# A scheduled attention and two-layer network kernel: later value loads in the planner's order, and the old state added on TensorE in early chunks

## The chip, the core and the metric

The kernel runs on one core of a Trainium2 chip. The metric is device microseconds of one execution, taken as the median of several runs. A core has TensorE (matmul, called PE in the profile, with PEld for its weight loads), VectorE (DVE), ScalarE (ACT), GpSimd (POOL) and SyncE (SP), which here does nothing but issue DMAs. Each engine works through its own list of instructions in the order in which the program wrote them. An instruction that waits for another engine or for a DMA holds up everything behind it on its own engine.

## What is computed

A linear attention with a state of 40x40 per head runs over 768 positions for 4 x 8 heads, and its output goes through two dense networks:

```python
for t in range(S):
    y[:, :, t] = np.einsum('bhd,bhde->bhe', rt, state)
    Sa = np.einsum('bhde,bhe->bhd', state, at)
    state_decay = state * wt[:, :, None, :] - np.einsum('bhd,bhe->bhde', Sa, bt)
    state = state_decay + np.einsum('bhd,bhe->bhde', vt, kt)
x = y.transpose(0, 2, 1, 3).reshape(B * S, H * D)              # 3072 x 320
h = np.maximum(np.maximum(x @ w1, x @ w2), x @ w3) @ w_out     # 768 wide
out = (h @ w_a * (h @ w_b)) @ w_out2                           # 1536 wide
```

## The kernel before

**Stages.** The 768 positions are cut into 24 chunks of 32, and two chunks make a pair (12 pairs). For each pair, `prep` loads decay factors, keys and the vectors a, scans the decays (L395, L399), multiplies keys and vectors by them, makes a block of products on TensorE (L446 for the first five pairs, L428 for the others), and solves small triangular systems on VectorE and GpSimd (`solve`, L500 to L502). Its results travel through DRAM because they change partitions. The products go out as BD and come back as BU for the solve (L460, L466). The first result goes out as TD and comes back as TT (L472, L476), the second out as ED and back as NB (L481, L484). All of these are DMAs in SP's queue.

**The chain.** `chain(c)` does chunk c, and each step needs the one before:

- z (L617, needs the operands ZR, which hold the state and a value load), then Zs on ScalarE (L623)
- "half" (L631, needs TT), then Zy on ScalarE (L635)
- u (L644, needs NB), then four copies into XX on ScalarE (L654)
- the state product (L664, function `smm`, two halves x = 0 and 1, 16 matmuls each, reads XX and YR)
- a VectorE add of the product to the state ST (L672), in every fourth chunk a VectorE multiplication of ST by a decay (L676), and copies from ST into ZR for the next z (L683 on ScalarE or L684 on VectorE, whichever the planner takes)

ST is also transposed on TensorE for the next chunk (L593). Off this chain the chunk's output is made by L690, L702, L706, L720 and L724. It goes to DRAM and comes back as xf (`gather`, L733 to L740).

**Dense networks.** `moe_a(p)` runs the first network on a pair (L828 and L853 to L857 on TensorE), writes X2D to DRAM (L863, L864), and needs weights split into two parts by `weights_a` (VectorE L750 to L753 and matmuls L777, L778, L780). `stage_b` splits the weights of the second network and stores them in DRAM. `moe_b` runs the second network in six tiles (L982 to L992) after all attention is done.

**Order.** Nothing is ordered by hand. Each step is handed to a planner (`Plan.op`) with its engine, an assumed duration, its operands and a priority. `Plan.run` plays all of this through on assumed durations and writes each engine's instructions in the order that comes out. The attention has the best priority, `moe_a` a lower one. For a DMA the planner assumes a time on SP, a time `lat` until its data is there, and a delay `pre` before SP may take it once its operands are free; these only decide the order, and no instruction waits for them on the chip. Where an operation has a second way (`alt`), the planner picks the engine. When the planner finds TensorE too idle for its clock it inserts a **fill**: a 128x128 matmul whose result nobody reads (`P.keep`, L276 in the profile). Fills stand in TensorE's list like any other work.

**Loads of a chunk.** `vload(d, 0)` loads values into ZR, `vload(d, 1)` loads values into XX (both L557). RB is L562, XT L564 and YL L568. Each overwrites what the previous chunk's matmuls still read, so SP's wait for such a load ends when that matmul is done.

Of the kernel before, what the change touches and what calls it, by code (L numbers as in the profile page):

```python
# [22 lines left out]
GP = [0, 64]  # L23
NYR, NZR = 2, 1
NW = 9
LV = 9
KG = 5
NSPL = 2
DMIN = 0.4
# [208 lines left out]
def body(nc, tc, ia, out_ap):  # L238
# [8 lines left out]
    def dv(n, ps=False):  # L247
        return 0.15 + n * 0.00105 if ps else 0.12 + n * 0.0014

    def ac(n):  # L250
        return 0.17 + n * 0.0009
# [2 lines left out]
        return 0.4 + n * 0.0023  # L254

    def dma(fn, nbytes, r=(), w=(), pri=0.0, pre=1.2):
        return op("SP", max(DMIN, nbytes / 300e3), fn, r=r, w=w, pri=pri, lat=2.0 + nbytes / 200e3, pre=pre)

    def adma(fn, nbytes, r=(), w=(), pri=0.0, after=()):

# [279 lines left out]
    def chain(c):  # L540
# [8 lines left out]
        def vload(d, q, after=()):  # L549

            for i in range(2):
                t, w = ((lambda i=i: (ZR[d % NZR][64 - GP[i]:96 - GP[i], i].rearrange("p u x d -> p (u x d)"), ia["vz"][d, i]), ("ZRv", d % NZR, i)),
                        (lambda i=i: (XX[64 * i:64 * i + 32].rearrange("p u g d -> p (u g d)"), ia["vx"][d, i]), ("XXv", i)))[q]
                if after:
                    adma(lambda w_, t=t: A.dma_start(*t()), 82e3, w=[w], pri=pr, after=after)
                else:
                    dma(lambda w_, t=t: SP.dma_start(*t()), 82e3, w=[w], pri=pr)  # L557

        vload(c, 0)
        for g in range(2):  # L560
            r0 = GP[g]
            dma(lambda w_, g=g, r0=r0: SP.dma_start(RB[40 * g:40 * g + 40, g].rearrange("p u t -> p (u t)"), ia["rb"][c, g]),  # L562
                82e3, w=[("RB", g)], pri=pr)
        dma(lambda w_: SP.dma_start(XT[0:80, :, 0, :], ia["vt"][c].rearrange("p (u t) -> p u t", t=32)),  # L564
            328e3, w=[("XTv", 0), ("XTv", 1)], pri=pr)
        for x in range(2):
            y0 = 64 * (1 - x)
            dma(lambda w_, x=x, y0=y0: SP.dma_start(YL[y0:y0 + 40, x].rearrange("p u g t -> p (u g t)"), ia["ry"][c, x]),  # L568
                82e3, w=[("YLr", x)], pri=pr)
        vload(c, 1)  # L570

        for hf in range(2):
# [84 lines left out]
        for x in range(2):  # L657
            pn = ("a", "s", c, x)

            def smm(w_, x=x, pn=pn):  # L660
                ps = bank[w_[pn]]
                for u in range(8):
                    for g in range(2):
                        T.matmul(ps[64 * g:64 * g + 40, u * 40:u * 40 + 40],  # L664
                                 Y_[64 * x:64 * x + 64, x, u, g], XX[64 * x:64 * x + 64, u, g], start=True, stop=True)

            if c == NCH - 1:
                continue
            op("PE", 0.82, smm, r=[("YRy", yb, x, hf) for hf in range(2)] + [("XXu", x, pq) for pq in range(2)] + [("XXv", x)],
               w=[pn], ps=[pn], act=0.22, pri=pr)  # L670
            sv = ST[0:104, :, 1 - x, 0:40]
            op("DVE", dv(320, True), lambda w_, sv=sv, pn=pn: V.tensor_tensor(  # L672
                sv, bank[w_[pn]][0:104, 0:320].rearrange("p (u d) -> p u d", d=40), sv, ALU.add),
               r=[pn], w=["ST", ("STx", x)], fin=[pn], pri=pr)
            if cc and p % 2:
                op("DVE", 0.74, lambda w_, sv=sv, x=x: V.tensor_tensor(  # L676
                    sv, sv, P_[0:104, cc].rearrange("p (u x) s -> p u x s", x=2)[:, :, x, 32:33].to_broadcast([104, 8, 40]), ALU.mult),
# [1 line left out]
            for g in range(2):  # L679
                r0 = GP[g]  # L680
                o_ = ZR[z2][r0:r0 + 40, g, :, 1 - x]
                i_ = ST[r0:r0 + 40, :, 1 - x, 0:40]
                op("ACT", ac(320), lambda w_, o_=o_, i_=i_: A.activation(o_, i_, AF.Copy), r=[("STx", x)], w=[("ZRs", z2, g)], pri=pr,  # L683
                   alt=[("DVE", 0.47, lambda w_, o_=o_, i_=i_: V.tensor_copy(o_, i_))])  # L684

        px = ("a", "xt", c)

# [575 lines left out]
```

## Time and profile before

| | |
|---|---|
| median of 3 runs | 1092.65 us (1087.15 to 1097.81) |
| the profiled execution, its own time | 1090.93 us |
| its span in the profile | 1088.7 us |
| mean granted TensorE clock | 0.975 |
| PE, DVE, ACT, POOL busy | 95%, 60%, 44%, 21% |
| instructions in the trace | 34319 |

The profile has one execution. The span runs from its first to its last instruction, and 2.2 us of its time lie outside the span. A busy PE in the profile can be doing fills. "Issue" is idle time for which the profile shows no cause.

### The profile page before, as it was taken

To read this page: it belongs to the slowest core of one execution; us is meant where nothing else is said; L and a number is where in the kernel's file an instruction comes from. 1 tells how busy PE (TensorE), PEld (TensorE's weight loads), DVE (VectorE), ACT (ScalarE), POOL (GpSimd) and SP (SyncE) were. 2 spreads that over 40 slices of the span, in tenths; PEclk is the share of its full clock that TensorE was granted. 3 is DMA by queue.
4 is the path that set the end of the run, shared out by engine and by line. 5 is a ranking of instruction groups with operands and counts; after the bars stand their busy time and mean duration, and the time that the engine had idled before them with its cause. 6 is when DMAs were issued, how large, how long until landed. Compare 5 with 4: busy or idle time off the path is not lost.

```text
span 1088.7 us, 34319 instructions
## 1 busy us (share of the span) xinstructions
PE 1034.9 (95%) x14868; PEld 936.6 (86%) x14868; DVE 654.0 (60%) x1091; ACT 480.7 (44%) x1115; POOL 230.1 (21%) x198
## 2 busy tenths in 40 slices
PE   8999789999899998999899999999999999999997
PEld 7878778988798888898889899988888888888886
DVE  7896698968797875989587633475223232332222
ACT  6246546555647373847375532343222232222221
POOL 4441365533423222323320200011000000000000
PEclk9998899899999989999899999999999999999999
DMA  8846875656666847577655547742002000000000
GB/s 272 199 96 161 173 158 126 157 140 167 158 167 153 190 117 189 136 168 166 150 135 149 136 122 204 200 104 62 10 1 54 1 25 1 2 25 1 25 1 27
DMA packets 173437, 123.10 MB, mean 113 GB/s; under 512 B 122464, under 2 KB 147168, under 8 KB 172320
## 3 DMA queue, kind: packets, MB, share of 16 engines
q1 hardware_dynamic: 170688, 116.41, 43.4%
q10 hardware_dynamic: 2592, 4.42, 1.2%
q8 instruction: 119, 1.95, 0.8%
q14 instruction: 38, 0.31, 0.1%
HBM read 93.07 MB, written 27.72 MB: 111 GB/s over the span
## 4 chain that ended last, share of the span: by engine, by line
PE 70%; DVE 12%; DMA 8%; issue 4%; SPq 3%; ACT 1%; POOL 1%; DVEq 0%; POOLq 0%; ACTq 0%
PE bank L982 24%; PE bank L828 11%; PE bank L992 4%; PE bank L990 4%; PE bank L991 4%; PE bank L276 3%; DMA NB<-ED 2%; PE bank L664 2%; PE bank L720 2%; PE bank L644 2%; PE bank L702 2%; PE bank L853 2%; PE bank L854 1%; PE bank L617 1%; PE bank L855 1%
## 5 line engine op out<-in xcount | busy, mean ns | idle before, releaser
L1000 DVE TENSOR_TENSOR bas<-bank,bas 128x512 f32<-128x512 f32 x72 | 49.7, 691 | 188.8 <-PE bank L982 179.8
L982 PE MATMUL bank<-bxhi,bw 128*128 128x512 f32 x576 | 156.3, 393 | 0.0
L982 PEld LDWEIGHTS bank<-bxhi,bw 128*128 128x128 f32 x576 | 106.2, 188 | 20.8
L999 ACT ACTIVATE bas<-bank 128x512 f32<-128x512 f32 x72 | 43.0, 598 | 148.2 <-PE bank L982 144.2
L1002 ACT ACTIVATE bgh<-bas 128x512 fp32r<-128x512 f32 x72 | 45.5, 633 | 125.5 <-DVE bas L1000 125.5
L828 PE MATMUL bank<-xhi,whi 128*128 128x256 f32 x432 | 95.5, 303 | 0.0
L843 DVE TENSOR_TENSOR hm<-bank,hm 128x512 f32<-128x512 f32 x72 | 49.5, 688 | 67.0 <-PE bank L828 66.1
L982 PE MATMUL bank<-bxlo,bw 128*128 128x512 f32 x288 | 89.8, 393 | 0.0
L992 PE MATMUL bank<-bo,bgl 128*128 128x320 f32 x288 | 89.0, 309 | 0.4 <-DVE bgl L1003 0.4
L990 PE MATMUL bank<-bo,bgh 128*128 128x320 f32 x288 | 89.0, 309 | 0.0
L991 PE MATMUL bank<-bo,bgh 128*128 128x320 f32 x288 | 88.9, 309 | 0.0
L828 PE MATMUL bank<-xlo,whi 128*128 128x256 f32 x432 | 88.5, 287 | 0.0
L828 PE MATMUL bank<-xhi,wlo 128*128 128x256 f32 x432 | 88.2, 286 | 0.0
L413 POOL TENSOR_TENSOR ZL<-ZL,Pp 64x512 f32<-64x512 f32 x44 | 58.7, 1334 | 85.4 <-DVE Pp L395 75.0
L1003 DVE TENSOR_TENSOR bgl<-bas,bgh 128x512 fp32r<-128x512 f32 x72 | 49.8, 691 | 43.0 <-ACT bgh L1002 42.8
L276 PE MATMUL bank<-con 128*128 128x128 f32 x494 | 69.2, 293 | 4.0 <-DMA con<-in_con_dram 2.8
L828 PEld LDWEIGHTS bank<-xhi,whi 128*128 128x128 f32 x432 | 67.6, 194 | 2.6
L276 PEld LDWEIGHTS bank<-con 128*128 128x128 f32 x494 | 62.9, 203 | 7.6 <-ACT bank L344 2.8
L828 PEld LDWEIGHTS bank<-xlo,whi 128*128 128x128 f32 x432 | 68.6, 195 | 0.0
L828 PEld LDWEIGHTS bank<-xhi,wlo 128*128 128x128 f32 x432 | 68.4, 195 | 0.0
L982 PEld LDWEIGHTS bank<-bxlo,bw 128*128 128x128 f32 x288 | 54.1, 188 | 12.2
L828 PE MATMUL bank<-xt,wt 128*128 128x256 f32 x216 | 62.0, 287 | 0.0
(181 smaller groups left out, 2446.0 us busy)
## 6 DMA issues: line engine op xcount, KB each, us to landing
wraw<-in_wpb_dram SPq DMA_DIRECT2D x18, 480.0 KB
KT<-in_kb_dram SPq DMA_DIRECT2D x20, 384.0 KB
Pp<-in_wf_dram SPq DMA_DIRECT2D x10, 528.0 KB
Rp<-in_wr_dram SPq DMA_DIRECT2D x10, 528.0 KB
wraw<-in_wpa_dram SPq DMA_DIRECT2D x12, 384.0 KB
bw<-WD SPq DMA_DIRECT2D x9, 512.0 KB
WD<-wraw ACTq DMA_DIRECT2D x18, 240.0 KB
WD<-wca SPq DMA_DIRECT2D x18, 240.0 KB
```

Source lines behind the costliest of these rows:

```text
L276: P.keep = lambda b: T.matmul(bank[b][:, 0:128], ident, ident, start=True, stop=True)
L413: op("POOL", po(512), lambda w_, cc=cc, g=g, r0=r0: G.tensor_tensor(Z_[r0:r0 + 64, cc, g], Z_[r0:r0 + 64, cc, g], P_[r0:r0 + 64, cc, :, 0: ...
L828: T.matmul(ps, w, x, start=(i == 0), stop=(i == 7))
L843: op("DVE", dv(512, True), lambda w_, pn=pn: V.tensor_tensor(f(hm), bank[w_[pn]], f(hm), ALU.max), r=[pn], w=["hm"], fin=[pn], pri=ep)
L982: T.matmul(ps, w, x, start=(k == 0), stop=(k == 7))
L990: T.matmul(o, gh[:, c], oh, start=ff == 0, stop=False)
L991: T.matmul(o, gh[:, c], ol, start=False, stop=False)
L992: T.matmul(o, gl[:, c], oh, start=False, stop=ff == 11)
L999: op("ACT", ac(512), lambda w_, j=j, pa=pa: A.activation(tb["as", j], bank[w_[pa]], AF.Copy), r=[pa], w=[("bas", j)], fin=[pa], pri=ep)
L1000: op("DVE", dv(512, True), lambda w_, j=j, pb=pb: V.tensor_tensor(tb["as", j], bank[w_[pb]], tb["as", j], ALU.mult), r=[pb], w=[("bas", j) ...
L1002: op("ACT", ac(512), lambda w_, j=j, k=k: A.activation(tb["gh", k], tb["as", j], AF.Copy), r=[("bas", j)], w=[("gh", k)], pri=ep)
L1003: op("DVE", dv(512), lambda w_, j=j, k=k: V.tensor_tensor(tb["gl", k], tb["as", j], tb["gh", k], ALU.subtract), r=[("bas", j), ("gh", k)], ...
```

## The change

Three things change in the program, and the planner then writes a new order for every engine.

- The planner's assumed time until a DMA's data is there goes from 2.0 us + bytes / 200 GB/s to 1.4 us + bytes / 250 GB/s, for all DMAs that SP issues. Loads of a chunk get a longer `pre`: values into ZR 2.5 us and into XX 6.0 us, RB and XT 4.0 us, YL 5.0 us, each 1.2 us before.
- In chunks 1 to 8 (`early`) the old state joins the product in the same PSUM bank: a matmul of the identity with ST (104 partitions x 320 columns) comes first, the 16 matmuls of each half add to it, and ScalarE copies the sum into ST. The VectorE add is gone there. Later chunks keep it.
- The copies from ST into ZR are always ScalarE's. VectorE no longer has them as a second way.

```diff
-        return op("SP", max(DMIN, nbytes / 300e3), fn, r=r, w=w, pri=pri, lat=2.0 + nbytes / 200e3, pre=pre)
+        return op("SP", max(DMIN, nbytes / 300e3), fn, r=r, w=w, pri=pri, lat=1.4 + nbytes / 250e3, pre=pre)
...
-                    dma(lambda w_, t=t: SP.dma_start(*t()), 82e3, w=[w], pri=pr)
+                    dma(lambda w_, t=t: SP.dma_start(*t()), 82e3, w=[w], pri=pr, pre=[2.5, 6.0][q] if d else 1.2)
...
-                82e3, w=[("RB", g)], pri=pr)
+                82e3, w=[("RB", g)], pri=pr, pre=4.0 if c else 1.2)
...
+            early = 0 < c < NACC
+            if early:
+
+                op("PE", 0.6, lambda w_, x=x, pn=pn: T.matmul(bank[w_[pn]][0:104, 0:320], ident[0:104, 0:104], ST[0:104, :, 1 - x, 0:40], start=True, stop=False, skip_group_check=True),
+                   r=["ST", ("STx", x), "con"], w=[pn], ps=[pn], act=0.9, pri=pr)
+            op("PE", 0.82, lambda w_, smm=smm, early=early: smm(w_, early), r=[("YRy", yb, x, hf) for hf in range(2)] + [("XXu", x, pq) for pq in range(2)] + [("XXv", x)],
+               w=[pn], ps=[] if early else [pn], act=0.22, pri=pr)
             sv = ST[0:104, :, 1 - x, 0:40]
-            op("DVE", dv(320, True), lambda w_, sv=sv, pn=pn: V.tensor_tensor(
-                sv, bank[w_[pn]][0:104, 0:320].rearrange("p (u d) -> p u d", d=40), sv, ALU.add),
-               r=[pn], w=["ST", ("STx", x)], fin=[pn], pri=pr)
+            if early:
+                op("ACT", ac(320), lambda w_, sv=sv, pn=pn: A.activation(sv, bank[w_[pn]][0:104, 0:320].rearrange("p (u d) -> p u d", d=40), AF.Copy),
+                   r=[pn], w=["ST", ("STx", x)], fin=[pn], pri=pr)
+            else:
+                op("DVE", dv(320, True), lambda w_, sv=sv, pn=pn: V.tensor_tensor(
+                    sv, bank[w_[pn]][0:104, 0:320].rearrange("p (u d) -> p u d", d=40), sv, ALU.add),
+                   r=[pn], w=["ST", ("STx", x)], fin=[pn], pri=pr)
...
-                op("ACT", ac(320), lambda w_, o_=o_, i_=i_: A.activation(o_, i_, AF.Copy), r=[("STx", x)], w=[("ZRs", z2, g)], pri=pr,
-                   alt=[("DVE", 0.47, lambda w_, o_=o_, i_=i_: V.tensor_copy(o_, i_))])
+                op("ACT", ac(320), lambda w_, o_=o_, i_=i_: A.activation(o_, i_, AF.Copy), r=[("STx", x)], w=[("ZRs", z2, g)], pri=pr)
```

In the changed file line numbers are 1 higher from L27 on and 9 higher from about L690 on; the state product is L665 there, the new matmul L673, a fill L277.

TensorE, chunk 2 (third chunk), from the fills ahead of u to the next chunk's z. Before:

```order
L276 MATMUL bank_64<-con 128x128 x7
L644 MATMUL bank_64<-Zy,NB_145 32x40 x32
L276 MATMUL bank_69<-con 128x128 x5
L664 MATMUL bank_69<-XX,YR_131 40x40 x16
L276 MATMUL bank_66<-con 128x128
L664 MATMUL bank_66<-XX,YR_131 40x40 x16
L690 MATMUL bank_65<-con,XU 80x128 x4
L276 MATMUL bank_70<-con 128x128
L593 MATMUL bank_70<-con,ST 128x104 x4
L593 MATMUL bank_68<-con,ST 128x104 x4
L702 MATMUL bank_63<-RB,XT 64x64 x16
L617 MATMUL bank_67<-ZR_136,ZL_127 32x40 x32
```

The same place with the change:

```order
L277 MATMUL bank_68<-con 128x128 x5
L645 MATMUL bank_68<-Zy,NB_145 32x40 x32
L277 MATMUL bank_70<-con 128x128 x5
L665 MATMUL bank_67<-XX,YR_131 40x40 x16
L277 MATMUL bank_70<-con 128x128
L699 MATMUL bank_70<-con,XU 80x128 x4
L673 MATMUL bank_63<-ST,con 104x320
L665 MATMUL bank_63<-XX,YR_131 40x40 x16
L711 MATMUL bank_65<-RB,XT 64x64 x16
L673 MATMUL bank_64<-ST,con 104x320
L594 MATMUL bank_68<-con,ST 128x104 x4
L618 MATMUL bank_67<-ZR_136,ZL_127 32x40 x32
```

Three fills are gone and two state matmuls (L673) are in, the first for the second half of this chunk, the second already for chunk 3.

SP's queue at pair 3 (fourth pair; BD_71 and BU are its products on the way to the solve, XX the values of chunk 5). Before:

```order
L460 DMA BD_71<-ZL_126 32x16x32
L740 DMA xf<-XD_81 64x256 x2
L760 DMA wraw<-in_wpa_dram 128x768
L460 DMA BD_71<-ZL_126 32x16x32
L375 DMA Rp<-in_wr_dram 128x1056
L460 DMA BD_71<-ZL_126 32x16x32 x2
L557 DMA XX<-in_vx_dram 32x640 x2
L466 DMA BU<-BD_71 64x512
L466 DMA BU<-BD_71 64x496
L564 DMA XT<-in_vt_dram 80x16x32
L562 DMA RB<-in_rb_dram 40x512 x2
```

With the change:

```order
L461 DMA BD_71<-ZL_126 32x16x32
L376 DMA Rp<-in_wr_dram 128x1056
L461 DMA BD_71<-ZL_126 32x16x32
L769 DMA wraw<-in_wpa_dram 128x768
L461 DMA BD_71<-ZL_126 32x16x32 x2
L749 DMA xf<-XD_81 64x256
L467 DMA BU<-BD_71 64x512
L467 DMA BU<-BD_71 64x496
L558 DMA XX<-in_vx_dram 32x640
L383 DMA ZL_128<-in_aa_dram 48x2x512 x2
L565 DMA XT<-in_vt_dram 80x16x32
L563 DMA RB<-in_rb_dram 40x512 x2
```

The value load XX moved from ahead of BU to behind it.

SP's queue at pair 5 (chunk 10 is its first), from TT to NB. Before:

```order
L476 DMA TT_141<-TD_76 32x16x32 x4
L375 DMA Pp_121<-in_wf_dram 128x1056
L375 DMA Rp<-in_wr_dram 128x1056
L738 DMA xf<-XD_80 128x2x256
L740 DMA xf<-XD_80 64x256 x2
L863 DMA X2D_85<-x2s 128x512
L864 DMA X2D_85<-x2s 64x256
L481 DMA ED_79<-TC 64x128 x2
L920 DMA wraw<-in_wpb_dram 128x960
L928 DMA WD<-wca 128x480
L460 DMA BD_71<-ZL_126 32x16x32 x2
L484 DMA NB_145<-ED_79 16x16x16 x4
```

With the change:

```order
L376 DMA Pp_121<-in_wf_dram 128x1056
L569 DMA YL<-in_ry_dram 40x512 x2
L937 DMA WD<-wca 128x480
L929 DMA wraw<-in_wpb_dram 128x960
L477 DMA TT_141<-TD_76 32x16x32 x4
L371 DMA KT_125<-in_kb_dram 48x2048
L482 DMA ED_79<-TC 64x128 x2
L371 DMA KT_125<-in_kb_dram 48x2048
L485 DMA NB_145<-ED_79 16x16x16 x4
```

Ten DMAs between TT and NB, besides ED, became two. Counted over TensorE's whole list, fills go from 247 to 193, 53 of the 54 before the z of chunk 5 (211 to 158), and 16 state matmuls are new, 9 of them before that z. Between "half" and u of chunk 10 stand 80 matmuls of L828 and 16 of L853 to L857 before; with the change 16, 16, and 16 of L428.

## Rows read from the trace of the kernel before

**Rows 1.** The page: busy time of each engine, share of the span, instructions.
```profile
PE 1034.9 (95%) x14868; PEld 936.6 (86%) x14868; DVE 654.0 (60%) x1091; ACT 480.7 (44%) x1115; POOL 230.1 (21%) x198
```

**Rows 2.** Stretches: length, PE, PEld, DVE, ACT, POOL busy, PEclk, DMA share, GB/s.
```profile
26.00:80.40 54.40, 50.67 (x746) 42.80 (x746) 47.88 (x83) 20.50 (x55) 24.61 (x21) 1.00 0.66 150
...
174.20:689.30 515.10, 484.90 (x9910) 454.94 (x9911) 382.22 (x642) 282.72 (x695) 148.86 (x127) 0.97 0.64 157
689.40:1088.70 399.30, 392.78 (x2018) 343.01 (x2016) 134.31 (x214) 108.44 (x188) 6.87 (x6) 0.99 0.11 30
```

**Rows 3.** What PE waited for, 0 to 650 us: total us, times, longest.
```profile
PE bank L644 <- DMA NB<-ED: 13.6, 9, 3.2
PE bank L631 <- DMA TT<-TD: 5.9, 11, 2.2
```

**Rows 4.** PE instructions by form: busy us, mean ns (a fill is two).
```profile
L276 PE MATMUL bank<-con 128*128 128x128 f32 x494 | 69.2, 293 | 4.0 <-DMA con<-in_con_dram 2.8 <-DVE XY L724 1.1
```

**Rows 5.** Timeline of PE, and its last row from the chain: start, us, what.
```profile
11.15 0.84 PE L777 MATMUL bank<-wraw,con 128*128 128x384 f32 x2
11.83 0.81 PE L778 MATMUL bank<-whi,x2s 128*128 128x384 f32 x2
...
47.48 6.86 PE L276 MATMUL bank<-con 128*128 128x128 f32 x60
...
90.93 0.59 PE L778 MATMUL bank<-woh,x2s 128*128 128x256 f32 x2
91.36 0.61 PE L780 MATMUL bank<-wraw,con 128*128 128x256 f32 x2
...
665.71 9.60 PE bank L828 x80
```

**Rows 6.** VectorE and ScalarE work on the state, by line: busy us, mean ns.
```profile
L672 DVE TENSOR_TENSOR ST<-bank,ST 104x320 f32<-104x320 f32 x46 | 22.4, 488 | 16.5 <-PE bank L664 16.1
L684 DVE COPY ZR<-ST 40x320 f32<-40x320 f32 x26 | 13.8, 529 | 0.8
L683 ACT ACTIVATE ZR<-ST 40x320 f32<-40x320 f32 x66 | 30.8, 466 | 19.8 <-DVE ST L672 13.6 <-DVE ST L676 5.2
L623 ACT ACTIVATE Zs<-bank 128x320 f32<-128x320 f32 x24 | 10.4, 435 | 6.2 <-PE bank L617 5.6
```

**Rows 7.** Timeline of PE and DVE around the state product of chunk 3.
```profile
130.34 0.81 PE L664 MATMUL bank<-XX,YR 64*40 64x40 f32 x32
...
129.21 2.40 DVE L751 SCALAR_TENSOR_TENSOR wraw<-wraw,wca 128x384 uint32<-128x384 uint32 x1
...
134.47 0.48 DVE L672 TENSOR_TENSOR ST<-bank,ST 104x320 f32<-104x320 f32 x1
```

**Rows 8.** What SP waited for, 25 to 645 us.
```profile
SPq L557 <- PE bank L664: 77.0, 33, 8.5
```

**Rows 9.** Timeline of SP at pair 3.
```profile
162.80 2.29 SPq L460 DMA_DIRECT2D BD<-ZL  x2
168.86 2.21 SPq L557 DMA_DIRECT2D XX<-in_vx_dram  x2
171.24 1.51 SPq L466 DMA_DIRECT2D BU<-BD  x2
```

**Rows 10.** Timelines of DVE, SP and PE at pair 5, from TC to u.
```profile
312.65 0.68 DVE L502 TENSOR_REDUCE TC<-TP 128x32 f32<-128x512 f32 x1
...
317.23 1.11 SPq L740 DMA_DIRECT2D xf<-XD  x2
...
319.58 1.23 SPq L481 DMA_DIRECT2D ED<-TC  x2
...
323.22 2.35 SPq L484 DMA_DIRECT2D NB<-ED  x4
...
327.00 1.36 PE L644 MATMUL bank<-Zy,NB 32*32 32x40 f32 x64 [0.90 <-DMA NB<-ED]
```

**Rows 11.** A stretch after a wait of PE for NB, columns as in rows 2.
```profile
534.90:541.60 6.70, 5.97 (x98) 5.49 (x100) 3.48 (x6) 3.43 (x8) 3.18 (x5) 0.52 0.37 67
```

More of the change, by code (lines that the diff above doesn't have):

```diff
@@ L25 @@
 NW = 9
+NACC = 9
 LV = 9
@@ L562, in chain @@
             dma(lambda w_, g=g, r0=r0: SP.dma_start(RB[40 * g:40 * g + 40, g].rearrange("p u t -> p (u t)"), ia["rb"][c, g]),
-                82e3, w=[("RB", g)], pri=pr)
+                82e3, w=[("RB", g)], pri=pr, pre=4.0 if c else 1.2)
         dma(lambda w_: SP.dma_start(XT[0:80, :, 0, :], ia["vt"][c].rearrange("p (u t) -> p u t", t=32)),
-            328e3, w=[("XTv", 0), ("XTv", 1)], pri=pr)
+            328e3, w=[("XTv", 0), ("XTv", 1)], pri=pr, pre=4.0 if c else 1.2)
         for x in range(2):
@@ L568, in chain @@
             dma(lambda w_, x=x, y0=y0: SP.dma_start(YL[y0:y0 + 40, x].rearrange("p u g t -> p (u g t)"), ia["ry"][c, x]),
-                82e3, w=[("YLr", x)], pri=pr)
+                82e3, w=[("YLr", x)], pri=pr, pre=5.0 if c else 1.2)
         vload(c, 1)
@@ L658, in chain, with smm @@
             pn = ("a", "s", c, x)
-            def smm(w_, x=x, pn=pn):
+            def smm(w_, early, x=x, pn=pn):
                 ps = bank[w_[pn]]
@@ L664, in smm @@
                         T.matmul(ps[64 * g:64 * g + 40, u * 40:u * 40 + 40],
-                                 Y_[64 * x:64 * x + 64, x, u, g], XX[64 * x:64 * x + 64, u, g], start=True, stop=True)
+                                 Y_[64 * x:64 * x + 64, x, u, g], XX[64 * x:64 * x + 64, u, g], start=not early, stop=True, skip_group_check=early)
             if c == NCH - 1:
                 continue
-            op("PE", 0.82, smm, r=[("YRy", yb, x, hf) for hf in range(2)] + [("XXu", x, pq) for pq in range(2)] + [("XXv", x)],
-               w=[pn], ps=[pn], act=0.22, pri=pr)
-            sv = ST[0:104, :, 1 - x, 0:40]
-            op("DVE", dv(320, True), lambda w_, sv=sv, pn=pn: V.tensor_tensor(
-                sv, bank[w_[pn]][0:104, 0:320].rearrange("p (u d) -> p u d", d=40), sv, ALU.add),
-               r=[pn], w=["ST", ("STx", x)], fin=[pn], pri=pr)
+            early = 0 < c < NACC
[4 more added lines that the diff above has]
+               w=[pn], ps=[] if early else [pn], act=0.22, pri=pr)
+            sv = ST[0:104, :, 1 - x, 0:40]
+            if early:
[5 more added lines that the diff above has]
+                   r=[pn], w=["ST", ("STx", x)], fin=[pn], pri=pr)
             if cc and p % 2:
```

## The prediction, made before the changed kernel ran

> **What bounds the kernel now.** I read the busy shares first. PE is busy 95% of the span [rows 1], but its list holds 247 fills, so that figure does not show that useful TensorE work sets the time. The table by stretch splits it. From 689.4 us on, the second network keeps PE busy 392.8 of 399.3 us with DVE, ACT and POOL far below; the change doesn't touch that part. In the attention, 174.2 to 689.3 us, PE is busy 484.9 of 515.1 us. In chunk 0, 26.0 to 80.4 us, DVE is busy 47.9 of 54.4 us, 88% [rows 2], and there the fills stand in PE's list. So early on VectorE and the chain of the solves set the pace and PE fills its time; later PE has first-network work waiting whenever the chain is held up, and the time is the sum of what stands in its list plus its waits. The list of waits names the largest two, DMAs each: 13.6 us for NB ahead of u and 5.9 us for TT ahead of "half" [rows 3].
>
> The sum is therefore made on PE: what its list loses, what it gains, and what its waits become. It starts from the profiled execution's own 1090.93 us. The median of the runs is 1092.65 us, 1.7 us more, and I add that at the end.
>
> **Fills.** 54 of 247 fills leave the list. All fills together take 69.2 us [rows 4], 0.280 us each. The cheapest stretch, 30 of them (60 instructions) in 6.86 us [rows 5], gives 0.229. So 54 x 0.280 = 15.1 us, at least 12.4. I take the mean over all of them. This gain is real only if what the fills waited for also comes sooner. It should: 20 of the 54 leave chunk 0 (94 to 74, counted between the z of chunks 0 and 1), where VectorE is the busy engine, and VectorE's list up to its first state add is 13 instructions shorter, since splitting of weights and some solve steps now stand behind it. If that cover is missing, the fills come back as idle time (a rival below).
>
> **The state matmul.** 16 come in, each two instructions over 320 columns, a form that the trace doesn't have. The nearest rows are the splitting matmuls. Over 384 columns the next one starts 11.83 - 11.15 = 0.68 us later, over 256 columns 91.36 - 90.93 = 0.43 us later [rows 5]. 320 lies midway, so 0.555 us each, 16 x 0.555 = 8.9 us, with ends at 6.9 and 10.9. Each stands ahead of its state product and needs only the old state, so it adds nothing to the chain, but it does take a place in PE's list.
>
> **Adds and copies.** VectorE loses 16 adds of 0.488 us (7.8 us) and 26 copies with 13.8 us in all [rows 6]. ScalarE gains 16 copies out of PSUM, priced by its copy of 128 x 320 out of PSUM at 0.435 us (7.0 us), and 26 copies of 0.466 us (12.1 us) [rows 6]: 480.7 us busy become about 500, 46% of the span. I cost these at nothing, because TensorE's list holds output or first-network matmuls between a state product and the next z. Without that cover, the copies that ran side by side on two engines and now follow each other cost up to 26 x 0.466 = 12.1 us. On the other side the early chunks no longer queue on VectorE. In chunk 3 the second state product ended at 130.34 + 0.81 = 131.15 us and its add began at 134.47, 3.3 us later, behind among others a 2.40 us splitting instruction [rows 7]. Chunk 3 still has its decay on VectorE, chunks 1, 2, 4, 5, 6 and 8 have not. This is part of what pays for the missing fills, so it isn't counted again.
>
> **Later loads.** SP waited 33 times, 77.0 us in all, for a state product to free XX [rows 8]. At pair 3 the last BD was issued by 165.09 us, then SP stood until the XX load at 168.86 and issued BU only at 171.24 [rows 9]. With BU ahead of XX, as the new list has it, BU can go when BD has landed. SP's waits cost nothing by themselves; they are worth what PE later waits for TT and NB. The bounds are 0 and the whole 13.6 + 5.9 = 19.5 us of rows 3. I take 0, since the same edit lets the planner move u closer to "half", which uses the gain up. Chunk 10 shows this. Between "half" and u stood 96 first-network matmuls, at 9.60 / 80 = 0.12 us [rows 5] 11.5 us; now there are 32 and 16 of L428, at the same price 5.8 us at most. So PE comes to u 5.7 us sooner, at about 327.00 - 0.90 - 5.7 = 320.4 us. The data: TC was done at 312.65 + 0.68 = 313.33, but ED was issued at 319.58, since the xf load ahead of it was issued only at 317.23; u began at 327.00 [rows 10]. If ED leaves at once, all behind it comes 6.2 us sooner and u can start at 320.8. PE would wait 0.4 us, where it waited 0.9.
>
> **Shorter assumed DMA time.** This edit only reorders. It does harm if the data really takes longer. After NB's last issue (323.22 + 2.35 = 325.57) u began within 1.43 us [rows 10]; the new assumption for that transfer of 16 KB is 1.4 + 0.06 us, so here it holds, at no cost. The Trainium skill, page "DMA: Bandwidth & Descriptors", section "Latency and other measured facts", speaks against the edit: it puts the fixed cost of a DMA at about 2 us, most of it access to HBM, which grows under load. By that figure u would start 0.6 us later than planned in each of 12 pairs, an estimated 7 us from the page, and the time would be about 1094 us. The row above came in below the page, but it is one place of twelve.
>
> **The sum.** 1090.93 - 15.1 + 8.9 = 1084.7 us; with the 1.7 us to the median, 1086.4. I predict **1086 us**. The ends of the two prices give 1084 to 1091.
>
> **Rivals.**
>
> *Waits shrink.* The lighter SP queue (ten DMAs between TT and NB at pair 5, ED aside, become two) frees more than the closer u uses. Half of the 19.5 us goes, 9.8 us. After such a wait PE ran at a granted 0.52, near the lower of its two clock levels, for 6.7 us [rows 11], 3.2 us lost each time; two such stretches less give 6.4. 1084.7 - 9.8 - 6.4 + 1.7 = 1070 us. For it: SP's long waits. Against it: the closer u.
>
> *u waits for NB (slower).* u is moved closer, but ED and NB still queue behind loads that aren't ready. By the same count as in chunk 10, u stands some 6 us closer to "half" in chunks 0, 10, 14, 18 and 22, and within 3 us of its old distance in the others. Where ED stays 6 us late as at pair 5, PE waits 5.7 us more. In four of the five that is 22.8 us, plus two more half-clock stretches, 6.4: 1084.7 + 29.2 + 1.7 = 1116 us; in two of them without a clock loss, 1098. It decides once ED is issued over 3 us after TC in three of the five. For it: 6.25 us at pair 5. Against it: in the new list hardly anything stands between TT and ED there. The page named above would bring this rival about by itself, in all pairs and at a lower price.
>
> *The fills were not the time.* VectorE and the solves before chunk 5 are no faster, and the 15.1 us return as idle time. The 9 state matmuls before chunk 5 fit into that idle time, the 7 later ones cost 3.9 us: 1090.93 + 3.9 + 1.7 = 1097 us. For it: part of the shorter plan is only an assumption. Against it: the adds and splits that leave the busy VectorE are real.
>
> *XX comes too late.* Loads that are issued later can hold up the next state product. SP issued two such loads in 2.21 us [rows 9], and the products of a pair's two chunks lie several chain steps apart, so I expect at most a microsecond in each of 12 pairs, and keep it in the upper part of the range.
>
> **How the numbers follow.** Chances: the forecast 0.46, waits shrink 0.24, u waits for NB 0.17, fills were not the time 0.13. A change of about 1%, beyond 1081.7 or 1103.6 us, is what a measurement of this kernel can tell from none. Faster takes the 0.24 and 0.04 of the forecast: 0.28. Slower takes 0.11 of the waits for NB and 0.01 of the forecast: 0.12. Same is left with 0.60. The range goes from just under the first rival to midway between the two prices of the second, 1069 to 1107, which leaves out some 0.17.
>
> **What would show each step.** PE's fills at 386 instructions and near 54 us. The state matmul's group near 0.55 us a piece. The z of chunk 5, which opens the stretch at 174.2 us in rows 2, some 10 us earlier; if it stays there with PE idle, the fills were not the time. SP's waits for L664 well under 77 us. PE's waits for NB and TT within some 5 us of 19.5 in all; far above, the slower rival; near 10, the faster one. The second network unchanged at 399 us. What would make the prediction wrong above all is a new wait in PE's list that none of these rows shows, since the planner has moved nearly every instruction.

## The result, and the profile after

The changed kernel took 1079.4 us (median of 5 runs, 1073.5 to 1093.9) against 1092.4 of the kernel before beside it: a ratio of 0.9868, 95% interval 0.9832 to 0.9903. A second measurement, run e1 below, gave 1080.5 us and 0.9907 (0.9880 to 0.9933). So it is about 1% faster, 10 to 14 us. The prediction was 1086 us, its range 1069 to 1107, with 0.60 on a change within 1% and 0.28 on faster. The time is in the range, 6 us below the figure. The first ratio lies just beyond the 1% on the faster side, the second just inside.

The ratios and intervals leave out executions in a slower state, such as the first profiled one of the changed kernel (1093.9 us) and one of e7 (2466.3 us), so the rows below are from the profile of e1.

The page of the changed kernel, busy time, share and instructions, answering [rows 1]:

```profile
PE 1033.2 (96%) x14792; PEld 927.8 (86%) x14792; DVE 642.5 (60%) x1035; ACT 498.7 (46%) x1157; POOL 253.8 (24%) x212
```

ACT gained 18.0 us, near the 19.1 of the working. DVE lost only 11.5 of the 21.6: the adds (14.5 us, [rows 6] had 22.4) and the copies (none, 13.8 before) did go, but the rest of its work takes 10.2 us more, with 14 instructions fewer. POOL's gain of 23.7 us goes with 14 more instructions, which the planner gave it in the new order.

The changed kernel by stretch, columns as in [rows 2]: up to the z of chunk 5, in it chunk 0 (from its z to that of chunk 1), then chunk 5 to the end of the attention, then the second network.

```profile
0.00:161.67 161.67, 151.23 (x2827) 129.40 (x2827) 128.72 (x219) 93.44 (x242) 67.28 (x59) 0.92 0.75 182
30.66:75.16 44.50, 44.03 (x688) 37.90 (x687) 37.09 (x71) 19.20 (x51) 14.99 (x13) 0.95 0.63 149
161.70:678.40 516.70, 487.37 (x9934) 453.46 (x9934) 377.61 (x606) 296.04 (x727) 178.91 (x144) 0.98 0.64 160
678.40:1079.10 400.70, 394.56 (x2035) 344.92 (x2033) 136.10 (x212) 109.16 (x189) 7.59 (x10) 1.00 0.10 28
```

The kernel before up to its z of chunk 5:

```profile
0.00:174.10 174.10, 156.98 (x2943) 138.46 (x2943) 137.35 (x236) 89.36 (x233) 74.23 (x66) 0.94 0.71 174
```

Chunk 0 is 9.9 us shorter (44.5, was 54.4), but its z comes 4.8 us later (30.7, was 25.9), so the z of chunk 1 comes some 5 us sooner. The z of chunk 5 comes at 161.7 us instead of 174.1. Of these 12.4 us, 5.7 are TensorE's busy time (151.2, was 157.0) and 6.7 its idle time (10.4, was 17.1). From there on nothing is gained: 516.7 us to the second network where it took 515.1, then 400.7 where it took 399.3. In these two executions the whole gain is made before chunk 5.

The chain itself goes on gaining. Its last z, the end of the range in the next rows (first row before, second with the change), comes 31 us sooner, but the second network starts only 11 us sooner:

```profile
L617 PE MATMUL bank<-ZR,ZL x1536: 197/202/225, 25.9 to 628.3; 128*32 128x40 f32 x192
L618 PE MATMUL bank<-ZR,ZL x1536: 197/202/277, 30.7 to 597.1; 128*32 128x40 f32 x192
```

First-network work left in TensorE's list takes up the difference: 432 instructions of L837 stand behind the last z, where 296 of L828 did. So in these two a chain that is ahead late in the attention shortens nothing by itself.

Groups of the changed kernel by form, TensorE's and then ScalarE's (busy us, mean ns), answering [rows 4, 6]:

```profile
L277 PE MATMUL bank<-con 128*128 128x128 f32 x386 | 57.9, 303 | 3.7 <-DMA con<-in_con_dram 2.9 <-DVE ZL L454 0.9
...
L673 PE MATMUL bank<-ST,con 104*104 104x320 f32 x32 | 13.1, 492 | 0.0
...
L693 ACT ACTIVATE ZR<-ST 40x320 f32<-40x320 f32 x92 | 43.1, 468 | 9.7 <-DVE ST L686 3.9 <-DVE ST L682 3.8
...
L679 ACT ACTIVATE ST<-bank 104x320 f32<-104x320 f32 x16 | 7.0, 435 | 4.6 <-PE bank L665 4.4
```

The waits of TensorE, 0 to 680 us, and of SP for a state product in the same stretch (total us, times, longest), answering [rows 3, 8]:

```profile
PE bank L632 <- DMA TT<-TD: 6.5, 9, 2.8
PE bank L729 <- DVE YL L715: 5.4, 4, 2.9
PE bank L645 <- issue: 4.1, 1, 4.1
...
PE bank L645 <- DMA NB<-ED: 3.3, 8, 1.7
```

```profile
SPq L558 <- PE bank L665: 7.5, 6, 3.3
```

SP's 77.0 us of waiting have become 7.5, and TensorE waits 9.8 us for NB and TT where it waited 19.5. At pair 3 BU now goes out ahead of the XX load, 5.1 us after the last BD, where [rows 9] had 6.2:

```profile
155.51 1.31 SPq L461 DMA_DIRECT2D BD<-ZL  x2
...
161.94 1.09 SPq L467 DMA_DIRECT2D BU<-BD  x2
163.13 0.53 SPq L558 DMA_DIRECT2D XX<-in_vx_dram  x1
```

### The profile page after: what moved, and what is told of

Its sections match the earlier page's. It is cut to its first block, busy times and chain, and to the rows that moved or that the text cites. A ratio compares the mean times of both kernels' runs of the same rounds, so it can differ in the third digit from the quotient of the medians.

```text
span 1092.1 us, 34136 instructions
## 1 busy us (share of the span) xinstructions
PE 1045.6 (96%) x14792; PEld 938.5 (86%) x14792; DVE 639.8 (59%) x1035; ACT 499.3 (46%) x1157; POOL 252.2 (23%) x212
## 4 chain that ended last, share of the span: by engine, by line
PE 56%; DVE 2%; DMA 2%; issue 1%; SPq 1%; ACT 0%; POOL 0%; ACTq 0%; DVEq 0%; POOLq 0%
PE bank L991 24%; PE bank L837 10%; PE bank L999 4%; PE bank L1000 4%; PE bank L1001 4%; PE bank L665 1%; PE bank L862 1%; PE bank L729 1%; PE bank L711 1%; PE bank L864 1%; PE bank L863 1%; PE bank L594 1%; PE bank L645 1%; PE bank L632 1%; PE bank L429 1%
## 5 line engine op out<-in xcount | busy, mean ns | idle before, releaser
L837 PE MATMUL bank<-xhi,whi 128*128 128x256 f32 x432 | 97.6, 309 | 0.2 <-issue 0.2
L837 PE MATMUL bank<-xhi,wlo 128*128 128x256 f32 x432 | 89.6, 290 | 0.0
L837 PE MATMUL bank<-xlo,whi 128*128 128x256 f32 x432 | 89.3, 289 | 0.0
L837 PEld LDWEIGHTS bank<-xhi,whi 128*128 128x128 f32 x432 | 68.9, 198 | 5.3 <-DVE wraw L760 1.6
L837 PEld LDWEIGHTS bank<-xhi,wlo 128*128 128x128 f32 x432 | 69.8, 198 | 0.0
L837 PEld LDWEIGHTS bank<-xlo,whi 128*128 128x128 f32 x432 | 69.8, 198 | 0.0
L837 PE MATMUL bank<-xt,wt 128*128 128x256 f32 x216 | 62.3, 288 | 0.8 <-issue 0.8
L837 PE MATMUL bank<-xl,wt 128*128 128x256 f32 x216 | 62.1, 287 | 0.0
L277 PE MATMUL bank<-con 128*128 128x128 f32 x386 | 57.2, 301 | 3.4 <-DMA con<-in_con_dram 2.8
```

What stands on the lines that cost most here:

```text
L277: P.keep = lambda b: T.matmul(bank[b][:, 0:128], ident, ident, start=True, stop=True)
L837: T.matmul(ps, w, x, start=(i == 0), stop=(i == 7))
```

## The experiments

Three explanations were to be told apart. **List**: the time is what stands in TensorE's list plus its waits, so fewer fills and shorter waits pay. **VectorE**: the early chunks queue on VectorE, so work that leaves it pays, or more narrowly the copies that z waits for. **Chain**: what counts is the direct path from a state product to the next z. Letters in the quoted expectations hold for that run only.

Ratios are against the kernel before on the same chip, with 95% intervals. The mean granted clock stands in each run's listing. As a bookkeeping aid I also give span x mean clock, averaged over a kernel's runs, minus the same of before, with 95% intervals: what the time would have changed at full clock throughout. It is an estimate, since it takes the whole span to stretch with TensorE's clock, and part of the span is other engines' work.

| run | what it is | ratio | span x clock, us | clock, own / before |
|---|---|---|---|---|
| e1 | the changed kernel | 0.9907 (0.9880 to 0.9933) | -10.2 ± 3.5 | 0.9745 / 0.9738 |
| e2 | DMA part alone | 1.0086 (1.0047 to 1.0125) | +3.2 ± 3.5 | 0.9717 / 0.9738 |
| e3 | state part alone | 0.9913 (0.9886 to 0.9940) | -7.2 ± 2.1 | 0.9786 / 0.9738 |
| e4 | before, 52 early fills left out | 1.0014 (0.9984 to 1.0044) | -6.3 ± 2.1 | 0.9668 / 0.9738 |
| e5 | after, early copies on VectorE | 0.9991 (0.9962 to 1.0020) | -3.7 ± 1.9 | 0.9672 / 0.9718 |
| e6 | after, state matmuls twice | 0.9914 (0.9888 to 0.9940) | -2.7 ± 2.7 | 0.9767 / 0.9718 |
| e7 | state matmul and copy alone | 0.9928 (0.9900 to 0.9957) | -0.7 ± 1.6 | 0.9763 / 0.9718 |
| e8 | before, order shaken | 1.0002 (0.9971 to 1.0033) | +3.3 ± 1.9 | 0.9750 / 0.9718 |
| e9 | after, only state copy on VectorE | 0.9924 (0.9900 to 0.9948) | -8.8 ± 1.6 | 0.9711 / 0.9737 |
| e10 | after, operands read from PSUM | 0.9952 (0.9924 to 0.9980) | -4.0 ± 2.5 | 0.9741 / 0.9737 |
| e11 | after, state part in all chunks | 1.0313 (1.0266 to 1.0361) | +23.6 ± 2.2 | 0.9650 / 0.9737 |
| e12 | operands on ScalarE alone | 1.0187 (1.0151 to 1.0223) | +4.0 ± 2.8 | 0.9603 / 0.9755 |

### Which part pays: e1, e2, e3

e1 is the changed kernel again. e2 keeps only the DMA edits (`lat` and the longer `pre`), e3 only the rest of the diff.

> The changed kernel once more, for a second profile beside the kernel before. The list theory (the time is what stands in TensorE's list: 54 fills fewer, 16 state matmuls more, waits as before) expects 1086 us with NB and TT waits near 19.5 us. The waits theory (SP's queue is lighter, so TT and NB come sooner) expects near 1079 us with these waits near 10 us, and SP's waits for the state product well under 77 us.

> The kernel before with the shorter assumed DMA time and the longer delays of the chunk loads, nothing else. Its list has 255 fills, 8 more than before. The list theory expects 1092 + 8 x 0.28 = 1095 us. The waits theory puts most of the gain here: 1080 to 1084 us. If only VectorE's relief pays, no change.

> The changed kernel with the old DMA assumptions: only the state matmuls of chunks 1 to 8 and the ScalarE copies are left of the change. 213 fills, 34 fewer than before, 16 state matmuls more. The list theory expects 1092 - 34 x 0.28 + 16 x 0.555 = 1092 us. The waits theory expects 1092 too, since SP's queue is not lighter. If VectorE's relief is what pays, 1080 to 1084 us.

The state part, with the order that the planner makes for it, has the whole gain (0.9913 against 0.9907 for both). The DMA part alone costs 0.9%, which none of e2's three expectations gave. It does what it says: in e2 TensorE's waits for NB and TT fall from 19.5 to 6.8 us.

```profile
PE bank L644 <- DMA NB<-ED: 5.6, 9, 3.5
...
PE bank L631 <- DMA TT<-TD: 1.2, 2, 1.0
```

The time does not follow in the median of e2 (1101.5 us). But this profile is of e2's fastest execution, 1087.0 us, so the waits of a typical one may be longer. e3 is the firmer case: with the old loads SP still waits 68.1 us for the state product and TensorE 12.4 us for NB and TT, and the time is that of the whole change. e1 came out as the waits theory said, 1080.5 us with 9.8 us of these waits, but e3 without the lighter queue did as well. So no gain from shorter waits is shown.

In e3's profile the z of chunk 1 comes at 81.0 us (80.5 before) and that of chunk 5 at 157.7, so there the gain before chunk 5 is made in chunks 1 to 4, where the state part acts. It too is e3's fastest execution (1069.9 us).

### The fills by themselves: e4

The kernel before in its own order. Only every fourth of the first 211 fills is left out:

```diff
-    P.keep = lambda b: T.matmul(bank[b][:, 0:128], ident, ident, start=True, stop=True)
+    fills = [0]
+
+    def fill(b):
+        fills[0] += 1
+        for _ in range(0 if fills[0] <= 211 and fills[0] % 4 == 0 else 1):
+            T.matmul(bank[b][:, 0:128], ident, ident, start=True, stop=True)
+    P.keep = fill
```

> The kernel before in its own order, with every fourth of its first 211 fills left out (52 fills; a fill's result is read by nobody). If the fills stood in TensorE's way, 52 x 0.28 = 14.6 us go: 1078 us. If they only fill a wait for VectorE and the solves, PE is idle in their place: 1090 to 1094 us, or more where the granted clock drops.

52 fills less, 14.6 us at the prediction's price, and no gain in time. The first 175 us of the kernel before and of e4, columns as in [rows 2]:

```profile
0.00:175.00 175.00, 157.88 (x3007) 139.30 (x3008) 138.25 (x238) 90.12 (x236) 75.13 (x66) 0.94 0.71 173
```

```profile
0.00:175.00 175.00, 155.13 (x2831) 134.19 (x2831) 136.89 (x235) 89.18 (x231) 74.30 (x66) 0.89 0.71 172
```

TensorE's busy time falls by only 2.8 us, the granted clock of this stretch falls from 0.94 to 0.89, and VectorE is no further at its end. Over all runs, span x clock falls by 6.3 us, 0.12 us a fill instead of 0.28, and the lower clock (0.9668 for 0.9738) would cost an estimated 1090 x 0.0070 / 0.974 = 7.8 us if all of the span went with it. Either the clock takes back what the list loses, or VectorE and the solves would have held the pace at any clock; e4 doesn't separate the two. Fills taken out alone, with nothing else sooner, gain no time.

### The order kept, the copies moved back: e5, e9

Both keep every engine's planned order. TensorE's list is the changed kernel's, instruction for instruction. Only the engine of copies in chunks 1 to 8 differs. e9 moves the 16 copies of the state:

```diff
-  lambda w_, sv=sv, pn=pn: A.activation(sv, bank[w_[pn]][0:104, 0:320].rearrange(...), AF.Copy),
+  lambda w_, sv=sv, pn=pn: V.tensor_copy(sv, bank[w_[pn]][0:104, 0:320].rearrange(...)),
```

e5 moves these and the 32 copies into the next operands:

```diff
-  lambda w_, o_=o_, i_=i_: A.activation(o_, i_, AF.Copy)
+  lambda w_, o_=o_, i_=i_, early=early: V.tensor_copy(o_, i_) if early else A.activation(o_, i_, AF.Copy)
```

> The changed kernel with the same planned order on every engine's queue, TensorE's instruction list identical, but in chunks 1 to 8 the 16 copies of the state out of PSUM and the 32 copies into the next operands are emitted on VectorE instead of ScalarE, at the places where ScalarE had them. VectorE gets 16 x 0.488 + 32 x 0.529 = 24.7 us back (prices of its add and of its copy in the kernel before; before it had 21.6 us of such work), the state matmuls stay. Theory A (freeing VectorE pays: in the first nine chunks VectorE sets the pace): the gain of the state part is lost, since the early chunks again queue on VectorE: 1080.5 + 8 to 20 = 1088 to 1100 us, the z of chunk 5 back near 172 us where it was 161.7, TensorE idle before it over 15 us. Theory B (what stands in TensorE's list sets the time): TensorE's list is the same, 1080.5 us within 0.3%, the z of chunk 5 within 2 us of 161.7.

> The changed kernel in the same planned order, but in chunks 1 to 8 only the 16 copies of the state out of PSUM are emitted on VectorE instead of ScalarE; the 32 copies into the next operands stay on ScalarE. The run with all 48 on VectorE gave 0.9991 of the kernel before, the changed kernel 0.9907 (or 0.9868 in its first measurement). VectorE gets 16 x 0.488 = 7.8 us of work back. Theory A1 (load on VectorE pays, in proportion to its us): 7.8 of 24.7 us, a third of the loss of 9.2: 0.993 to 0.994. Theory C (the copy of the state stands in the chain and VectorE's queue holds it up; the copies into the operands are of no account): nearly all of the loss, 0.997 to 1.000. Theory E (the copies into the operands are what mattered, they are two thirds of the work and stand nearest to the next z): no loss, 0.990 to 0.991.

e5 loses the whole gain: 0.9991 against 0.9907, (0.9991 - 0.9907) x 1091 = 9.2 us, within some ±4.3 by the two intervals. Its signs came too: the z of chunk 5 at 169.0 us in its profile, TensorE idle for 16.2 us before it. But e9's profile, its slowest execution, has them too (169.6 and 16.7 us), so they don't tell the two apart. e9 loses 0.0017, 1.9 ± 3.9 us, so theory C, that nearly all would be lost, falls. Between e9 and e5 lie 0.0067, 7.3 ± 4.1 us, for the copies into the next operands. That these matter more in kind is not shown: in e5 they take 20.2 us of VectorE and the state's copies 7.7, and 9.2 us shared out in proportion (theory A1) gives 6.7 and 2.5, as near to the measured. One place shows how a moved copy can delay z. The changed kernel, second half of chunk 1's state product (start, us):

```profile
87.94 0.81 PE L665 MATMUL bank<-XX,YR 64*40 64x40 f32 x32
...
88.79 0.44 ACT L679 ACTIVATE ST<-bank 104x320 f32<-104x320 f32 x1 [0.38 <-PE bank L665]
89.26 0.95 ACT L693 ACTIVATE ZR<-ST 40x320 f32<-40x320 f32 x2
...
92.10 0.86 PE L618 MATMUL bank<-ZR,ZL 128*32 128x40 f32 x64
```

The same in e5, PE, POOL and DVE:

```profile
89.01 0.81 PE L665 MATMUL bank<-XX,YR 64*40 64x40 f32 x32
...
90.49 1.92 POOL L501 TENSOR_TENSOR TP<-BU,TU 128x512 f32<-128x512 f32 x1 [2.19 <-DVE TC L503]
...
90.33 0.32 DVE L693 COPY ZR<-ST 40x320 f32<-40x320 f32 x1
90.56 0.48 DVE L762 SCALAR_TENSOR_TENSOR wraw<-wraw,wca 128x320 f32<-128x320 uint32 x1
91.08 1.52 DVE L693 COPY ZR<-ST 40x320 f32<-40x320 f32 x1
92.61 0.69 DVE L454 TENSOR_TENSOR ZL<-bank,con 64x512 f32<-64x512 f32 x1
...
94.64 0.47 DVE L679 COPY ST<-bank 104x320 f32<-104x320 f32 x1
...
96.47 0.71 PE L618 MATMUL bank<-ZR,ZL 128*32 128x40 f32 x54 [0.67 <-DVE ZR L693]
```

On ScalarE the state's copy begins 0.04 us after the product's end (88.75), both operand copies are done at 90.21, and z begins at 92.10 without a wait. On VectorE the product ends at 89.82, but the copy waits behind the first half's operand copies, a splitting step, two masking steps (L454) and two reductions of the solve until 94.64, and z's last part begins at 96.47. Over e5's attention z waited ten times, a wait that the changed kernel does not have:

```profile
PE bank L618 <- DVE ZR L693: 8.3, 10, 1.8
```

Neither run is the way back to the kernel before. e5 puts all 32 early operand copies on VectorE at places planned for ScalarE; the planner had given VectorE 11 of them, 8 in e7 below. VectorE's operand copies from the z of chunk 1 to that of chunk 9, before, e7 and e5 (length, DVE busy):

```profile
80.46:283.26 202.80, 7.53 (x11) 0.92 0.65 154
80.92:266.22 185.30, 4.93 (x8) 0.90 0.70 160
76.45:274.97 198.52, 19.88 (x31) 0.00 (x0) 0.91 0.67 154
```

And before, no wait of z for such a copy is listed. Nor did the 16 adds of chunks 1 to 8 queue for long: from a product's end to the start of its add it is 8.0 us in all, 4.9 of them in chunk 3. With the change it is 3.4 us, in e5 26.7 and in e9 24.5. Chunk 2, second half, before and in e9:

```profile
110.30 0.81 PE L664 MATMUL bank<-XX,YR 64*40 64x40 f32 x32
111.16 0.49 DVE L672 TENSOR_TENSOR ST<-bank,ST 104x320 f32<-104x320 f32 x1 [0.24 <-PE bank L664]
```

```profile
109.94 0.81 PE L665 MATMUL bank<-XX,YR 64*40 64x40 f32 x32
113.28 0.26 DVE L759 TENSOR_SCALAR wca<-wraw 128x192 uint32<-128x192 uint32 x1 [4.20 <-DMA wraw<-in_wpa_dram]
...
115.02 0.47 DVE L679 COPY ST<-bank 104x320 f32<-104x320 f32 x1
```

So e5 and e9 show what copies cost behind VectorE's list of the new order. What the change gained over the old order they don't show, and e9's 24.5 us of queueing went with 1.9 ± 3.9 us of time.

### What the state matmul costs: e6

```diff
-  lambda w_, x=x, pn=pn: T.matmul(..., ident[0:104, 0:104], ST[0:104, :, 1 - x, 0:40], ...)
+  lambda w_, x=x, pn=pn: [T.matmul(..., ident[0:104, 0:104], ST[0:104, :, 1 - x, 0:40], ...) for _ in range(2)]
```

> The changed kernel with each of the 16 state matmuls issued twice; the second overwrites the bank with the same values, so the result is unchanged and TensorE's list is longer by 16 pairs of instructions. The prediction's sum prices one at 0.555 us. Theory B (TensorE's list sets the time): +8.9 us, 1089.4 us. Theory A (early on TensorE has slack, VectorE and the chain set the pace): the matmuls of chunks 1 to 4 and part of the rest go into idle time; +0 to 4 us, 1080.5 to 1084.5 us, with the z of chunk 5 at most 1 us later than 161.7 and TensorE's idle time before it shorter by 2 to 5 us of 10.4.

```profile
L673 PE MATMUL bank<-ST,con 104*104 104x320 f32 x64 | 22.4, 475 | 0.0
```

The group grew by 22.4 - 13.1 = 9.3 us, 0.58 us for each of the 16 more. The ratio is that of the changed kernel, 0.9914 to 0.9907, +0.8 ± 4 us. By span x clock it is -2.7 to -10.2, +7.5 ± 4.4 us, which the higher clock (0.9767 against 0.9718 of before on that chip) offsets. In time theory A's 0 to 4 us came out, and theory B's 8.9 lies outside. Theory A's signs did not: in e6's profile the z of chunk 5 came 7.1 us later, and TensorE's idle time before it was 11.8 us, no shorter than 10.4. One profile is weak for this, since in e9's, without the doubled matmuls, that z came 7.9 us later. So the matmuls cost nearly their price by span x clock and little in time. With e1 and e6 on two chips, that they bring the better clock, as fills seem to, is not shown.

### Half of the state part, and the luck of an order: e7, e8, e12

e7 adds to the kernel before the state matmul and ScalarE's copy, e12 only takes away the second way of the operand copies. e8 changes one planner number:

```diff
-LAT = {"PE": 0.2, "ACT": 0.15, "DVE": 0.14, "POOL": 0.08}
+LAT = {"PE": 0.201, "ACT": 0.15, "DVE": 0.14, "POOL": 0.08}
```

> The kernel before with one half of the state part alone: the state matmul and ScalarE's copy out of PSUM for chunks 1 to 8. The next operands may still be copied by VectorE, the DMAs' assumed times and places in order are those of before. 237 fills by this plan (247 before, 213 with both halves). The run with both halves and without the DMA part gave 1080.9 us against 1091.1. Theory A (freeing VectorE pays in proportion): 16 adds of 0.488 us, 7.8 us, leave VectorE, of 21.6 us that both halves take away: about a third of the gain of 10.2, 1086 to 1089 us. Theory C (the chain pays: the state matmul takes the add out of the path and the rest is of no account): all of the gain, near 1081 us. Theory D (the new order alone, whatever moved, makes such differences): anywhere within 1081 to 1097.

> The kernel before with nothing changed but one number of the planner, its assumed TensorE latency 0.200 -> 0.201 us. No work is added or taken out, except that the plan now holds 264 fills instead of 247, and many instructions change places. This measures how far the time moves by a new order alone. Theory D (luck of the order): over 0.5% away from 1091.1 us, to either side, which would put the gains of 0.9% in doubt. Theories A and C: within 0.4% of 1091.1, 1086.7 to 1095.5 us. By the prediction's price of a fill, 17 more give 17 x 0.280 = +4.8 us, 1095.9; by the run that left 52 fills out and gained nothing, none.

> The kernel before with the other half of the state part alone: the copies into the next operands go to ScalarE only (26 of them were VectorE's, 13.8 us); the state is still added on VectorE from the bank, no state matmul, DMAs as before. 244 fills by this plan (247 before). Theory A (relief of VectorE pays, whatever work it is): 13.8 of the 21.6 us that the whole state part takes from VectorE, whose gain was 0.9% (0.9913): 0.993 to 0.996. Theory F (the state matmul with the copy on ScalarE is what pays; it alone gave 0.9928, and with the copies added 0.9913): the copies are worth the rest, 0.998 to 1.000. Theory G (ScalarE now does in sequence what two engines did side by side, at the end of the chain): slower, 1.002 to 1.011 (26 x 0.466 = 12.1 us at most).

e7 alone gives 0.9928 (0.9900 to 0.9957), in its middle most of the gain; the interval reaches from all of it to near the third that a share by VectorE's microseconds would be. By span x clock it gains nothing (-0.7 ± 1.6), so by this bookkeeping its gain is clock. e12 alone takes more work off VectorE (13.8 us against 7.8) and is 1.9% slower, beyond even theory G, the slowest of its expectations. So "work that leaves VectorE pays, whatever it is" falls as a rule. e12 runs at the lowest mean clock of all. One place in its profile, 380.0 to 384.2 us, and the stretch behind it (columns as in [rows 2]):

```profile
384.20:394.40 10.20, 6.36 (x107) 5.75 (x108) 8.33 (x7) 4.43 (x12) 6.91 (x5) 0.51 0.57 167
380.00:384.20 4.20, 1.56 (x11) 1.16 (x10) 3.94 (x6) 0.74 (x2) 2.53 (x2) 0.97 0.97 156
```

TensorE was busy 1.56 of 4.20 us, and the next 10.2 us ran at 0.51, near the lower of its two levels. Of e12's 21 us, an estimated 1092 x 0.0152 / 0.96 = 17 are clock by this bookkeeping. e8 shows that a new order without an edit can leave the time unchanged within 0.3%, with 17 fills more. It is one such order and no bound for others, and e12's order is a new one too. Why that order has so many holes stays open.

### Two attempts at a faster version: e10, e11

e10 lets the operand copies of chunks without decay read the product's bank, ahead of the state's copy. e11 sets `NACC = 23`, so that the state part holds in chunks 1 to 22.

```diff
+  if early and not dec:
+      zc = [... A.activation(ZR[...], bank[w_[pn]][r0:r0 + 40, 0:320]..., AF.Copy) for each g ...]
+      op("ACT", ac(320), ... A.activation(sv, bank[w_[pn]]..., AF.Copy), ..., after=zc)
```

> The changed kernel with one thing more: in the chunks 1, 2, 4, 5, 6 and 8, which have no decay, ScalarE's copies into the next operands read the state product's bank itself, and the copy of the state follows behind them, so that between the product and the next operands one ScalarE copy of 0.435 us less stands in the chain for each half; the plan is made anew and holds 232 fills. Theory C (the chain from the state product to the next z pays): 12 copies leave the path, in pairs that partly overlap, 3 to 5 us faster than the changed kernel: 0.986 to 0.988 of the kernel before where the changed kernel is 0.9907. Theory A (only VectorE's load pays): as the changed kernel, 0.989 to 0.992. The list theory of the prediction (39 fills more, 39 x 0.280 = 10.9 us): 1.000.

> The changed kernel with the state matmul and ScalarE's copy in all chunks from 1 to 22 instead of 1 to 8: 28 more state matmuls, 28 VectorE adds of 0.488 us (13.7 us) less. The plan is made anew and holds 226 fills. Theory A (VectorE's load pays wherever VectorE is busy, in the trace to about 510 us): some 13.7 x 0.4 = 5 us faster than the changed kernel, 0.986 of the kernel before. List theory (from chunk 5 on the time is what stands in TensorE's list): 28 x 0.555 = +15.5 us, 1.005. Between them (early only, later neither pays): 0.989 to 0.993.

Neither beats the changed kernel. In e10 a shorter chain gave nothing (0.9952 against 0.9907), against the chain explanation as far as one new order can tell. Span x clock is 6.2 us above the changed kernel's, part of the 10.9 us that the list would charge for its 39 further fills. e11 is 4% slower than the changed kernel. Its groups:

```profile
L673 PE MATMUL bank<-ST,con 104*104 104x320 f32 x88 | 34.1, 470 | 0.7 <-DVE YL L715 0.7
...
L277 PE MATMUL bank<-con 128*128 128x128 f32 x452 | 65.8, 299 | 4.9 <-DMA con<-in_con_dram 2.9 <-ACT YR L603 1.2 <-ACT ST L679 0.5
```

State matmuls and fills take 21.0 + 7.9 = 28.9 us more than in the changed kernel, most of the 33.8 us that span x clock rose, and the lower clock adds some 10 us. In this order VectorE's relief late in the attention buys nothing, and what TensorE's list grew by counts nearly in full.

## Why the prediction was right, and which terms were mis-sized

**The bound.** That the second network would not move and that TensorE's list counts later held: 400.7 us at the end, 516.7 us before it although the chain ran 31 us ahead, and e11. The gain came where the prediction put it. By its prices, 53 fills less and 9 state matmuls more give -9.8 us before the z of chunk 5, the other fill and 7 matmuls +3.6 up to the second network, and 0 in it; measured are -12.4, +1.6 and +1.4. That VectorE sets the pace early is argued: the state part shortened chunks 1 to 4 in e3, but e12 took more off VectorE and lost.

**Fills, -15.1 us: the right place, another cause.** The group came out at 386 instructions, as announced, and 57.9 us, 11.3 less. The working let this count only if what the fills waited for came sooner too, and it did, 12.4 us at the z of chunk 5. But the price is not the fills' own. e4 took 52 away and nothing else, and gained nothing in time. What pays is whatever made the z come sooner, for which the sum had no term; the fills' time stood in for it. The rival that the fills were not the time was right on this, and wrong that the time would return as idle time: TensorE's idle time before that z fell from 17.1 to 10.4 us.

**State matmul, +8.9 us: mis-sized in time.** On the list e6 gives 0.58 us for one more, where 0.555 was said; the changed kernel's own group has 13.1 / 16 = 0.82 us busy for each, above the sign. In the time, e6 finds 0.8 ± 4 us.

**Adds and copies, 0: not settled.** The working costed them at nothing "because TensorE's list holds output or first-network matmuls between a state product and the next z". On ScalarE this held: no wait of z for such a copy is listed for e1. With the same TensorE list but the copies on VectorE, e5 pays 9.2 us and z waits. That is no measure of what the change gained here, since VectorE had 11 of these 32 copies before, its adds had waited 8.0 us in all, and the operand copies alone (e12) made it slower. The prediction's 3.3 us in chunk 3 [rows 7] was the longest of the 16, and 1.5 us of it were the chain's own add and decay of the first half.

**Later loads, 0 in time: right.** e1 and e3 agree with and without them. The signs moved far (77.0 to 7.5 us on SP, 19.5 to 9.8 on TensorE), near the 10 that was to announce the faster rival, yet the state part alone, with the old loads, has the same time. So that rival's mechanism came about and its price, 9.8 + 6.4 us, did not.

**Shorter assumed DMA time, 0.** u did not come to wait more: 3.3 us of waits for NB in all, where 13.6 stood. The slower rival is out. The row that the prediction leaned on is weaker than it says: its 1.43 us count from the end of NB's last issue. From that issue's start it is an estimated 1.43 + 2.35 / 4 = 2.0 us, so the row doesn't show that the time is under 2 us. Why the DMA part alone is 0.9% slower stays open.

**How much was luck.** The sum gave -6.2 us, and -10.6 (e1) to -13.0 were measured. The place of the gain was foreseen. The size came near because the two wrong prices, a gain for the fills and a full cost for the state matmuls, partly offset each other, and that was luck.

**Left open.** Which part of the state part carries the gain, and by which wait, is not shown. e4, e5, e6 and e9 keep the order of a kernel, so what they show is the edit. e2, e3, e7, e10, e11 and e12 each run in an order of their own, and what of their times is the edit and what the new order wasn't separated. One order without an edit (e8) left the time unchanged, and one with a small edit (e12) cost 1.9%, so a lucky order remains a rival for the gain of 1%. Against it: four orders with the early state matmul (e1, e3, e7, e10) were faster, and three without it (e2, e8, e12) were not.

## What to carry to other kernels

An instruction that only keeps TensorE busy may not be worth its duration when it goes: take some out alone and look at the granted clock before it enters a sum. To price a copy that the next step of a chain needs, move it alone with the order held, and compare its wait with the one that it had before the change, not only with the moved one. Where a planner makes a new order for every edit, one run per edit can't tell the edit from the order. Shorter waits in a profile are no gain until the time says so.

## What the runs showed of the hardware

**Time and granted clock move together between runs of one kernel.** In 20 runs of the kernel before beside e1, the mean granted clock lay between 0.965 and 0.982 and the span between 1096.1 and 1084.7 at these ends; a straight line through the 20 falls 8.1 us for each 0.01 and accounts for about half of the spread (correlation -0.72). Which of the two moves the other isn't shown. A comparison of a per cent needs many runs of both kernels.

**A VectorE copy can take five times its usual time beside GpSimd.** e5's 32 operand copies:

```profile
L693 DVE COPY ZR<-ST 40x320 f32<-40x320 f32 x32 | 20.2, 631 | 0.6
```

The 15 that ran beside no busy GpSimd instruction took 0.31 to 0.32 us each. Of the 17 that met one, the 6 that had begun before it took their usual 0.29 to 0.33 us, and the 11 that began while it ran took 0.74 to 1.63 us. In the rows of e5 above, the copy at 91.08 lasted until 92.60, and the GpSimd instruction that was under way ended at 92.41. The Trainium skill, page "Advanced Engine Details and Errata", section "VectorE Performance Modes", says that the second SBUF port of VectorE is shared with GpSimd and that GpSimd instructions and two-port VectorE instructions block each other. These rows agree on the blocking; that these copies use two ports no row shows. ScalarE's copies (0.468 us on average) and VectorE's copies out of PSUM (0.48 us, as at 94.64) kept their times. So the mean of 0.529 us in [rows 6] was a mix: 21 of the 26 took 0.31 to 0.33 us, 5 took 0.88 to 2.34. A copy that looks cheap on VectorE is not where GpSimd is busy.
